# The order of every engine's work written out as a table instead of worked out by a planner

## The chip, the core and the metric

The kernel runs on one core of a Trainium2 chip. A core has a matrix engine (PE, with its weight loads shown as PEld), a vector engine (DVE), a scalar engine (ACT), a general engine (POOL) and a queue engine that issues transfers (SP). Each runs its own list of instructions in order and waits on semaphores for the others. The metric is the device time of one execution in microseconds, lower is better; the times shown are medians.

## The reference, cut to what matters

```python
def reference(**kwargs):
    attn_out = _attn_ref(q, k, v)             # 4 batches, 8 heads, 576 tokens, 64 wide, float32
    x = attn_out.transpose(0, 2, 1, 3).reshape(2304, 512)
    x = _moe_ref(x, w_in, w_out)              # 512 -> 2048 -> 512
    return _moe2_ref(x, w_gate, w_val, w_out, rms_g)   # 512 -> 1536 -> 512

def _attn_ref(q, k, v):
    scores = q @ k.T / sqrt(64)               # a query sees keys of its own and earlier blocks of 64
    attn = softmax(masked scores)
    return attn @ v

def _moe_ref(x, w_in, w_out):
    h = x @ w_in
    return (h * tanh(softplus(h))) @ w_out    # mish

def _moe2_ref(x, w_gate, w_val, w_out, rms_g):
    xn = x / sqrt(mean(x * x) + 1e-6) * rms_g
    g = xn @ w_gate
    return (g * sigmoid(g) * (xn @ w_val)) @ w_out
```

## The kernel before

Most products are made of float16 pairs: a float32 matrix is split into a high and a low half, and three of the four products of halves are added in PSUM (`PASSES`). Three stages overlap. In the first, attention runs tile by tile (`a1_0` is batch 1, tile 0 of 128 tokens): scores `s` (L988, L989 for the mask), their row maxima (DVE L1023), a bias (L1032), the exponential `e` (ACT L1048), a split into halves `p` (L1122, L1125, L1129), a transposing transfer to `pt`, the product with `v` (PE L1162), and a scaled copy `xfl` (DVE L1192) that empties the PSUM tile. In the second stage, interleaved with the first, the mish layer runs in steps of 256 columns by 256 tokens: `h` (PE L1379) into a ring of two PSUM tiles, mish `f` on ACT (L1405), its halves `g` (L1417 or L530 or L1414, then L1422), and `y` (PE L1440). The third stage multiplies `g` and `v` (PE L1841) and `o` (PE L2000) by a seven-product scheme, with sums and differences on DVE or POOL (L1884, L1897) and halves `pp` (L1907, L1908, L1910); its weights are prepared in halves beforehand (L1687 to L1698).

ACT holds one table of functions at a time. Exponential, mish and silu need different ones, so each turn from `e` to `f` or back puts an ACT_TABLE_LOAD into ACT's list.

The code first records 5,150 operations, each with the buffers it reads and writes and one to three alternatives: an engine, a duration in ns, and the function that emits it. Nothing is emitted while recording. `Plan.run` then calls `place`, a list scheduler with a cost model (latencies between engines, table loads, the shared lock of DVE and POOL), and emits the operations in the order of the start times found, each on the engine found; seven tables of numbers shift its priorities. `with_idle` puts fillers before PE operations where the plan has PE idle in the first 60 us: matmuls of zeros that nothing reads (L2086). The order of emission sets the order on every engine, all transfers going through SP.

```python
for o in self.with_idle():
    o.alts[o.pick][2]()
```

Of the kernel before, what the change touches and what calls it, by code (L numbers as in the profile page):

```python
# [26 lines left out]
LAT = {  # L27
    PE: {PE: 0, ACT: 200, DVE: 200, POOL: 240, DMA: 200, NONE: 0},
    ACT: {PE: 153, ACT: 133, DVE: 133, POOL: 180, DMA: 127, NONE: 0},
    DVE: {PE: 131, ACT: 112, DVE: 112, POOL: 160, DMA: 106, NONE: 0},  # L30
    POOL: {PE: 87, ACT: 68, DVE: 68, POOL: 113, DMA: 62, NONE: 0},
    DMA: {PE: 640, ACT: 660, DVE: 660, POOL: 700, DMA: 650, NONE: 0},
    NONE: {PE: 0, ACT: 0, DVE: 0, POOL: 0, DMA: 0, NONE: 0},
}
T_TINY, TINY_AP = 75.0, 52.0
T_DGE, T_DGE_HEADS, T_BUS = 660.0, 720.0, 1250.0
T_DGE_P16, T_DGE_X16, T_DGE_KT, T_DGE_QT, T_DGE_XN = 1330.0, 1330.0, 1450.0, 1370.0, (1400.0, 1950.0)
T_TABLE, TABLE_PULL = 1290.0, 2500.0
WINDOW, HEAT, COOL = 3413.33, 0.9, 0.3
FILL, FILL_SHARE = 60000.0, 0.75  # L40
HOLD = {DVE: 100.0, POOL: 90.0}
# [46 lines left out]


def shares(e, ns):  # L90
    return e == POOL or e == DVE and type(ns) is Shared
# [8 lines left out]
class Plan:  # L100
# [43 lines left out]
    def place(self, key, back=False):  # L144


        ops = self.ops
        n = len(ops)
        free = {e: 0.0 for e in (PE, ACT, DVE, POOL, DMA, NONE)}
        warm, win, busy, bus = True, 0, 0.0, 0.0  # L150
        later = {e: [] for e in free}
        now = {e: {} for e in free}
        table, lock = None, 0.0
        start, end = [None] * n, [0.0] * n
        ready = [[0.0] * len(o.alts) for o in ops]
        wait = [len(o.succ) if back else len(o.deps) for o in ops]

        def arrive(i):
            o = ops[i]
            for z in (o.pick,) if back else (self.picks[i],) if i in self.picks else range(len(o.alts)):  # L160
                e = o.alts[z][0]
                heapq.heappush(later[e], (ready[i][z], key[i], i, z))

        for i in range(n):
            if wait[i] == 0:
                arrive(i)
        left = n
        while left:
            best = None
            for e in free:  # L170
                w, q, f = later[e], now[e], free[e]
                while w and w[0][0] <= f:
                    t, p, i, z = heapq.heappop(w)
                    kind = ops[i].table if e == ACT else shares(e, ops[i].alts[z][1])
                    heapq.heappush(q.setdefault(kind, []), (p + 0.3 * z, i, z))
                first = None
                for kind, h in q.items():
                    while h and start[h[0][1]] is not None:
                        heapq.heappop(h)
                    if h:  # L180
                        pull, t = 0.0, f
                        if back:
                            pass
                        elif e == ACT:
                            pull = 0.0 if kind is None or kind == table else TABLE_PULL
                        elif kind and lock - HOLD[e] > f:
                            t = lock - HOLD[e]
                            pull = t - f
                        if first is None or h[0][0] + pull < first[0]:
                            first = h[0][0] + pull, t, h  # L190
                while w and start[w[0][2]] is not None:
                    heapq.heappop(w)
                if first is not None and (first[1] <= f or not w or first[1] <= w[0][0]):
                    c = (first[1], e, first[2])
                elif w:
                    c = (w[0][0], e, None)
                else:
                    continue
                if best is None or c[:2] < best[:2]:
                    best = c  # L200
            t, e, heap = best
            if heap is not None:
                _, i, z = heapq.heappop(heap)
            elif e in HOLD and not back:
                free[e] = t
                continue
            else:
                _, _, i, z = heapq.heappop(later[e])
            o = ops[i]
            o.pick = z  # L210
            ns = o.alts[z][1]
            if e == ACT and o.table is not None and not back:
                if table is not None and table != o.table:
                    t += T_TABLE
                table = o.table
            start[i], end[i] = t, t + ns
            if not back and shares(e, ns):
                lock = end[i] = max(t + ns, lock + ns - HOLD[e])
            if e == PE and not back:

                x = t
                while ns > 0:
                    while x >= (win + 1) * WINDOW:
                        share = busy / WINDOW if win * WINDOW > FILL else 1.0
                        warm = share > COOL if warm else share > HEAT
                        win, busy = win + 1, 0.0
                    rate = 1.0 if warm else 2.0
                    step = min(ns * rate, (win + 1) * WINDOW - x)
                    x, busy, ns = x + step, busy + step, ns - step / rate
                    if ns < 1e-6:  # L230
                        break
                end[i] = x
            free[e] = end[i]
            if e == DMA:
                free[e] = t + o.issue
                bus = end[i] = max(t + T_BUS + ns - ns.queued, bus) + ns.queued
            left -= 1
            for d in o.deps if back else o.succ:
                j = d.idx
                r = ready[j]  # L240
                if back:
                    r[d.pick] = max(r[d.pick], end[i] + LAT[d.alts[d.pick][0]][e])
                else:
                    for z, a in enumerate(d.alts):
                        r[z] = max(r[z], end[i] + LAT[e][a[0]])
                wait[j] -= 1
                if wait[j] == 0:
                    arrive(j)
        self.length = max(end)
        return start, end  # L250

    def run(self):
        for o in self.ops:
            for d in o.deps:
                d.succ.append(o)
        def inherit(key):

            for i in range(len(self.ops) - 1, -1, -1):
                o = self.ops[i]
                if o.prio < URGENT:  # L260
                    key[i] = min(key[i], o.prio - URGE)
                for d in o.deps:
                    if key[d.idx] > key[i]:
                        key[d.idx] = key[i]
            return key

        key = inherit([o.prio for o in self.ops])
        best = None

        def rounds(key, n):  # L270
            nonlocal best
            for z in range(n + 1):
                start, end = self.place(key)
                if best is None or self.length < best[0]:
                    best = self.length, start, [o.pick for o in self.ops], end, key
                if z < n:
                    _, end = self.place([-t for t in end], True)
                    key = inherit([-t for t in end])

        rounds(key, ROUNDS)  # L280
        if SHIFT:
            self.picks = PICK
            rounds([k + SHIFT.get(o.part, 0.0) + FINE.get(o.idx, 0.0) for k, o in zip(best[4], self.ops)], ROUNDS2)
        self.length, start, picks, end, _ = best
        for i, o in enumerate(self.ops):
            o.start, o.pick, o.end = start[i], picks[i], end[i]
        for o in self.with_idle():
            o.alts[o.pick][2]()

    def with_idle(self):  # L290

        last = 0.0
        for o in sorted(self.ops, key=lambda o: (o.start, o.idx)):
            if o.alts[o.pick][0] == PE:
                if last < FILL:
                    for _ in range(int((o.start - last) * FILL_SHARE / t_mm(128) * (1.0 if last else 0.5))):
                        self.idle()
                last = o.end
            yield o


# [34 lines left out]
def block_attention_mish_mlp_gated_mlp(  # L336
# [16 lines left out]
    P = 128  # L353
    BLK = 64
    NBLK = S // BLK
    NPAIR = H // 2
# [1735 lines left out]
    close_pool("m1")  # L2092


ROUNDS = 20
URGENT, URGE, ROUNDS2 = 3000.0, 50000.0, 0
SHIFT = {
# [244 lines left out]
```

## Time and profile before

| | |
|---|---|
| median of 3 runs | 938.07 us (937.89 to 938.23) |
| profiled execution, first to last instruction (its span) | 935.2 us |
| PE busy | 911.7 us, 97% |
| DVE busy | 804.6 us, 86% |
| ACT busy | 643.0 us, 69% |
| POOL busy | 508.3 us, 54% |
| granted TensorE clock | 1.000 |

The profile gives the profiled execution its span alone; the median lies 2.9 us above it, for what comes before the first and after the last instruction. A matmul counts as busy from its start to the end of its result, and matmuls overlap in the engine, so a short wait between two of them can lie under the tail of the first.

### The profile page before, as it was taken

How to read it: one execution, taken by the hardware profiler on the slowest of the kernel's cores; microseconds unless marked ns; L12 is line 12 of the kernel's file. 1: busy time of each engine (PE TensorE's matmuls, PEld its weight loads, DVE VectorE, ACT ScalarE, POOL GpSimd, SP SyncE). 2: the span in 40 equal slices, each digit the busy share in tenths (PEclk: the TensorE clock that was granted, in tenths of full speed). 3: DMA queues.
4: the chain of work that ended last, by engine and by line, in shares of the span. 5: the costliest groups of instructions: out<-in, count | busy, mean ns of one | idle time of the engine just before them, and what ended most of it. 6: DMA issues, size and time to landing. Idle time of an engine off the chain costs nothing.

```text
span 935.2 us, 20362 instructions
## 1 busy us (share of the span) xinstructions
PE 911.7 (97%) x7395; PEld 622.2 (67%) x7396; DVE 804.6 (86%) x1920; ACT 643.0 (69%) x1330; POOL 508.3 (54%) x644
## 2 busy tenths in 40 slices
PE   8999998999999999999999999999999999999997
PEld 7775567476676766676675665767676676767676
DVE  6899978988786669989874989999999999997676
ACT  4687969899689788887795457667675465463431
POOL 1172548585655526578532749388757577353311
PEclk9999999999999999999999999999999999999999
DMA  9676596888958595898944667736566370716011
GB/s 240 188 232 186 136 172 138 141 146 168 161 117 150 112 169 119 162 184 180 180 71 87 133 184 145 176 76 105 91 187 117 104 131 14 139 21 154 13 69 68
DMA packets 317189, 125.47 MB, mean 134 GB/s; under 512 B 296352, under 2 KB 296352, under 8 KB 317088
## 3 DMA queue, kind: packets, MB, share of 16 engines
q1 hardware_dynamic: 317088, 124.17, 62.6%
q8 instruction: 58, 0.95, 0.4%
q14 instruction: 43, 0.35, 0.1%
HBM read 50.07 MB, written 12.98 MB: 67 GB/s over the span
## 4 chain that ended last, share of the span: by engine, by line
PE 41%; DVE 11%; ACT 5%; POOL 3%; DMA 2%; issue 2%; SPq 0%; DVEq 0%; ACTq 0%; POOLq 0%
PE o L2000 10%; PE y L1440 6%; PE g_u L1841 6%; PE v_u L1841 5%; PE h L1379 4%; PE g L1841 4%; PE v L1841 4%; DMA pt<-p 1%; PE shared L1162 1%; DVE g L1422 1%; DVE mx L1023 1%; ACT e L1048 1%; DVE pp L1910 1%; DVE w2o L564 0%; PE s L988 0%
## 5 line engine op out<-in xcount | busy, mean ns | idle before, releaser
L1379 PE MATMUL h<-x,w1i 128*128 128x256 f16 x1536 | 181.4, 273 | 2.0 <-ACT f L1405 1.8
L1440 PE MATMUL y<-w1o,g 128*128 128x512 f16 x768 | 179.4, 379 | 0.1
L1379 PEld LDWEIGHTS <-w1i 128*128 128x128 f16 x1536 | 145.7, 98 | 25.2 <-issue 3.9
L2000 PE MATMUL o<-w2o,pp 128*128 128x256 f16 x1134 | 138.0, 272 | 1.0 <-POOL pp L1910 0.6
L2000 PEld LDWEIGHTS <-pp 128*128 128x128 f16 x1134 | 110.7, 98 | 23.5 <-issue 1.1
L1440 PEld LDWEIGHTS <-g 128*128 128x128 f16 x768 | 70.4, 98 | 75.4 <-issue 1.7
L1841 PEld LDWEIGHTS <-w2g 128*128 128x128 f16 x756 | 73.8, 98 | 48.1 <-issue 3.8
L1841 PEld LDWEIGHTS <-w2v 128*128 128x128 f16 x756 | 73.9, 98 | 46.0 <-issue 1.8
L1023 DVE TENSOR_REDUCE mx<-s 128x1 f32<-128x512 f32 (+4 forms) x128 | 70.2, 557 | 19.3 <-PE s L989 13.7
L1048 ACT ACTIVATE e<-s,bias,cS 128x512 f32<-128x512 f32 (+4 forms) x120 | 72.6, 607 | 20.1 <-DVE bias L1032 6.9
L1841 PE MATMUL v_u<-xnT,w2v 128*128 128x384 f16 x432 | 81.1, 326 | 0.1
L1841 PE MATMUL g_u<-xnT,w2g 128*128 128x384 f16 x432 | 79.6, 326 | 0.1
L1129 POOL TENSOR_TENSOR p<-e,p 128x384 f16<-128x384 f32 (+4 forms) x60 | 58.6, 977 | 36.4 <-ACT p L1125 19.7
L1422 DVE SCALAR_TENSOR_TENSOR g<-f,ich,g 128x512 f16<-128x512 f32 x64 | 56.7, 886 | 17.1 <-ACT g L1417 10.8
L1841 PE MATMUL g<-xnT,w2g 128*128 128x384 f16 x324 | 61.3, 326 | 1.2 <-DVE sl21g L1878 0.8
L1162 PEld LDWEIGHTS <-pt 128*128 128x128 f16 (+1 forms) x1368 | 44.5, 103 | 26.6 <-issue 10.7
L1841 PE MATMUL v<-xnT,w2v 128*128 128x384 f16 x324 | 61.5, 326 | 0.6 <-DVE u2v L1922 0.6
L1162 PE MATMUL shared<-v,pt 128*128 128x64 f16 (+1 forms) x1368 | 50.5, 195 | 5.5 <-DMA pt<-p 2.6
L1048 ACT ACT_TABLE_LOAD x41 | 52.6, 1283 | 2.5 <-DVE p L1129 1.0
L1405 ACT ACTIVATE f<-h,ch 128x512 f32<-128x512 f32 x64 | 43.4, 685 | 9.2 <-PE h L1379 4.8
L1405 ACT ACT_TABLE_LOAD x38 | 48.8, 1283 | 1.1 <-PE h L1379 0.4
L530 POOL TENSOR_SCALAR p<-e 128x128 f16<-128x128 f32 (+2 forms) x55 | 29.2, 534 | 27.5 <-ACT e L1048 21.1
(351 smaller groups left out, 2070.2 us busy)
## 6 DMA issues: line engine op xcount, KB each, us to landing
wir<-in_moe_w_in_dram SPq DMA_DIRECT2D x16, 512.0 KB, 5.2
wor<-in_moe_w_out_dram SPq DMA_DIRECT2D x16, 512.0 KB, 3.8
w2rg<-in_moe_w_gate_dram SPq DMA_DIRECT2D x24, 256.0 KB, 3.5
w2rv<-in_moe_w_val_dram SPq DMA_DIRECT2D x24, 256.0 KB, 3.3
w2ro<-in_moe_w_out_dram SPq DMA_DIRECT2D x24, 256.0 KB, 2.8
q<-in_q_dram SPq DMA_DIRECT2D x16, 256.0 KB, 3.9
k<-in_k_dram SPq DMA_DIRECT2D x16, 256.0 KB, 4.1
v<-in_v_dram SPq DMA_DIRECT2D x16, 256.0 KB, 3.8
```

What stands on the lines that cost most here:

```text
L530: nc.gpsimd.tensor_scalar(out=out_, in0=in_, scalar1=by, scalar2=1.0, op0=ALU.mult, op1=ALU.mult)
L1023: lambda z=z, cols=cols: nc.vector.reduce_max(out=mx()[:, cols], in_=ts[z](), axis=AX.X),
L1048: lambda y=y, z=z, c0=c0, w=w, acc=acc, e=e, h=h: nc.scalar.activation(out=e()[:, c0 : c0 + w], in_=ts[z]()[:, y, :], func=AF.Exp, bias=bi ...
L1129: lo = lambda eng, z=z, ev=ev: eng.tensor_tensor(out=view(p16)[:, z, :, 1, :], in0=ev(0, kt), in1=view(p16)[:, z, :, 0, :], op=ALU.subtract)
L1162: nc.tensor.matmul(xt()[sl, cols, :], pv(z)[:, t, ph, sl], v16[b, t]()[:, vh, c0 : c0 + D], start=(t == 0 and y == 0), stop=(t == kt - 1 a ...
L1379: nc.tensor.matmul(ph()[:, g, :], w1i[fq]()[:, cc, wh, f * P : (f + 1) * P], x()[:, xh * NCC + cc, :], start=(z == 0), stop=(z == 3 * NCC ...
L1405: ACT, t_act(W, 1, True), lambda: nc.scalar.activation(out=e(), in_=phf(), func=AF.Mish, scale=cs()),
L1422: lambda: nc.vector.scalar_tensor_tensor(out=g16()[:, 1], in0=hv(), scalar=sc(), in1=g16()[:, 0], op0=ALU.mult, op1=ALU.subtract),
L1440: nc.tensor.matmul(yps[t, m](), g16()[:, gh, g, m * P : (m + 1) * P], w1o[f]()[:, wh, :], start=(f == 0 and z == 0), stop=(f == NF1 - 1 an ...
L1841: nc.tensor.matmul(b(), w[wo]()[:, wh, cc, :], x()[:, (2 * xo + xh) * 2 + cc, :], start=(first and i == 0), stop=(i == 5), skip_group_chec ...
L1910: lo = lambda eng: eng.tensor_tensor(out=pp()[:, 1, :], in0=x(), in1=pp()[:, 0, :], op=ALU.subtract)
L2000: nc.tensor.matmul(b()[:, side, :], pps[r][po]()[:, gh, m * P : (m + 1) * P], w[wo]()[:, wh, r, :], start=(first and i == 0), stop=(i == 5 ...
```

## The change

The planner is taken out. `run` walks a table `ORDER` of the 5,150 operation numbers, emits each on the engine that a string `PICKS` names, and puts `IDLE` fillers before eleven of them. The operations, their buffers and their dependencies are the same, except that the ten transposes of `q` and `k` for batch 0 also wait for two constants that the fillers read. Lines of the kernel body stand 167 lines earlier in the changed file (L1379 becomes L1212).

```diff
     def run(self):
-        for o in self.ops:
-            for d in o.deps:
-                d.succ.append(o)
...
-        for o in self.with_idle():
-            o.alts[o.pick][2]()
+
+        for i in ORDER:
+            for _ in range(IDLE.get(i, 0)):
+                self.idle()
+            self.ops[i].alts[int(PICKS[i])][2]()
...
-        op(PE, t_mm(P, 2) * NPAIR, mm, r=[t, ident], w=[tp], at=at)
+        op(PE, t_mm(P, 2) * NPAIR, mm, r=[t, ident, idle_in, ones_h], w=[tp], at=at)
...
+ORDER = (
+    29, 34, 2, 17, 20, 23, 40, 35, 8, 1, 3, 36, 18, 5, 37, 19, 26, 6, 9, 10, 7, 38, 46, 21, 30, 22, 159, 52, 158, 24,
...
+PICKS = (
+    "0000000000000000000000000100000000000000000010000010000010000000000001000000000001000000000000000000"
...
+IDLE = {
+    18: 36, 21: 13, 159: 11, 164: 3, 187: 4, 216: 9, 168: 1, 185: 1, 255: 1, 272: 8, 277: 4,
+}
```

Of the 3,548 operations on DVE, ACT and POOL, 716 change their engine: 264 from POOL to DVE and 186 back, 98 from ACT to DVE and 87 back, 50 from POOL to ACT and 31 back. DVE goes from 1,920 operations to 2,009, POOL from 639 to 542, ACT from 989 to 997. Among the operations recorded for the third stage and its weights alone, DVE goes from 809 to 886 and POOL from 236 to 167. ACT's list has 63 table loads instead of 85. The fillers go from 156 to 91; the first transpose of `q` has 36 ahead of it instead of 25, and from the second attention group on 31 stand in place of 107. Three places follow; in the names, numbers behind the tile's own are buffer numbers.

**SP at the program's start.** Before (`wir` is a raw piece of `w_in`):

```order
L755 DMA q_0_2_88<-in_q_dram 128x8x64
L755 DMA k_0_3_109<-in_k_dram 128x8x64
L755 DMA v_0_7_125<-in_v_dram 128x8x64
L579 DMA wir_0_127<-in_moe_w_in_dram 128x1024
L579 DMA wir_1_129<-in_moe_w_in_dram 128x1024
```

Changed:

```order
L412 DMA wir_0_90<-in_moe_w_in_dram 128x1024
L588 DMA q_0_2_97<-in_q_dram 128x8x64
L588 DMA k_0_3_99<-in_k_dram 128x8x64
L588 DMA k_1_4_101<-in_k_dram 128x8x64
L412 DMA wir_1_103<-in_moe_w_in_dram 128x1024
```

A weight piece now goes ahead of the first queries and keys.

**DVE where batch 0's last attention tile is copied out of PSUM** (`xfl0_4_0`, which reads the tile that batch 1's first product with `v` will write). Before, from the scale of batch 1's `v` on:

```order
L708 TENSOR_SCALAR s2_2309<-E1_496,wor_217_1284,wos_216_2304 128x4
L564 SCALAR_TENSOR_TENSOR v16_1_0_2284<-v1_0_157_1486,sv1_2268,v16_1_0_2284 128x512
L1188 TENSOR_SCALAR r_196_1991<-r_196_1991,fx0_4_2297 128x4
L559 TENSOR_SCALAR w1o0_2321<-wos0_971,s2_2309 128x512
L1192 TENSOR_TENSOR xfl0_4_0_2328<-shared_133,r_196_1991 128x256
```

Changed:

```order
L541 TENSOR_SCALAR s2_2178<-E1_751,wor_217_2172,wos_216_2176 128x4
L1021 TENSOR_SCALAR r_196_2174<-r_196_2174,fx0_4_2159 128x4
L386 TENSOR_TENSOR q16_1_2_1979<-q1_2_225_1746,q16_1_2_1979 128x8x64
L1019 RECIPROCAL r_212_2199<-r0_211_2044 128x4
L1025 TENSOR_TENSOR xfl0_4_0_2201<-shared_114,r_196_2174 128x256
L1255 SCALAR_TENSOR_TENSOR g11_2197<-f11_2108,ich1_1154,g11_2197 128x512
L776 COPY fxd_209_2225<-F2_2098 64x1
L397 SCALAR_TENSOR_TENSOR v16_1_0_2166<-v1_0_157_1494,sv1_2095,v16_1_0_2166 128x512
```

The low half of `v` stood ahead of the copy and now stands behind it, and the weight's high half (L559) is no longer among DVE's rows; on PE, 79 matmuls instead of 25 lie between the square sum of batch 1's `v` and the first product that reads its halves (48 of them of `h`, against 12).

**ACT between two mish steps of the same token tile** (`f25` and `f26`). Before:

```order
L1405 ACTIVATE f25_4110<-h25_4034,ch3_3372 128x512
L1417 ACTIVATE g25_4124<-f25_4110,ich3_3388 128x512
L1478 ACTIVATE sums_b_2995,ss_359_4128<-y2_1_3156,kap2_3386 128x512
L1048 ACT_TABLE_LOAD
L1048 ACTIVATE e2_0_0_4171,sum_345_4172<-s2_0_0_0_4052,bias_344_4130,cS_325_3552 128x128
L1405 ACT_TABLE_LOAD
L1405 ACTIVATE f26_4222<-h26_4087,ch3_3372 128x512
```

Changed:

```order
L1238 ACTIVATE f25_3919<-h25_3855,ch3_2813 128x512
L958 ACTIVATE p16_1_4_2_3849<-e1_4_2_3770 128x128
L1250 ACTIVATE g25_3923<-f25_3919,ich3_3414 128x512
L1311 ACTIVATE sums_b_2962,ss_359_3972<-y2_1_3109,kap2_3512 128x512
L1238 ACTIVATE f26_3998<-h26_3906,ch3_2813 128x512
L1348 ACTIVATE sums_b_2962<-sums_b_2962 128x3x256
L1250 ACTIVATE g26_4027<-f26_3998,ich3_3414 128x512
```

One exponential with a table load on either side stood between the two mish steps; it has moved behind `f27`, to its neighbours.

## Rows read from the trace of the kernel before

**Rows 1.** The page's part on engines: busy us, share of the span, instructions.

```profile
PE 911.7 (97%) x7395; PEld 622.2 (67%) x7396; DVE 804.6 (86%) x1920; ACT 643.0 (69%) x1330; POOL 508.3 (54%) x644
```

**Rows 2.** Busy time by stretch: length, engines (instructions), PE clock, DMA share, GB/s.

```profile
core 0: us, PE busy (x) PEld busy (x) DVE busy (x) ACT busy (x) POOL busy (x), PEclk, DMA share, GB/s
0.00:38.00 38.00, 33.72 (x305) 28.04 (x306) 26.20 (x79) 20.72 (x65) 5.25 (x22) 1.00 0.85 218
38.00:135.00 97.00, 96.83 (x588) 60.09 (x588) 91.25 (x213) 74.81 (x172) 45.58 (x67) 1.00 0.68 183
135.00:250.00 115.00, 108.66 (x1079) 73.03 (x1081) 99.34 (x320) 102.99 (x217) 76.22 (x108) 1.00 0.83 151
250.00:500.00 250.00, 244.79 (x2412) 168.16 (x2407) 202.95 (x560) 207.00 (x393) 136.22 (x199) 1.00 0.74 145
500.00:850.00 350.00, 347.32 (x2428) 234.63 (x2427) 324.56 (x646) 208.45 (x430) 225.84 (x231) 1.00 0.56 115
850.00:936.00 86.00, 80.41 (x599) 58.21 (x596) 60.33 (x106) 29.03 (x55) 19.20 (x18) 1.00 0.20 65
```

**Rows 3.** Waits of PE, whole span: who ended them, us in total, times, longest.

```profile
PE s L988 <- ACT e L1048: 3.3, 9, 0.7
PE shared L1162 <- DMA pt<-p: 2.6, 5, 0.9
PE shared L1162 <- DVE xfl L1192: 2.4, 2, 1.9
...
PE h L1379 <- ACT f L1405: 1.8, 3, 1.1
```

**Rows 4.** PE's groups by form: count, busy us, mean ns of one, idle before.

```profile
L1379 PE MATMUL h<-x,w1i 128*128 128x256 f16 x1536 | 181.4, 273 | 2.0 <-ACT f L1405 1.8
...
L2086 PE MATMUL shared<-idle_in,ones_h 128*128 128x128 bf16 x156 | 14.0, 242 | 2.5 <-DVE idle_in L451 1.9 <-DVE xfl L1192 0.5
```

**Rows 5.** The chain that ended last: start, us, one piece of many matmuls.

```profile
331.55 2.62 PE h L1379 x24
```

**Rows 6.** Timeline at 154 us: start, us, instruction, [idle before it and its releaser].

```profile
153.80 0.95 DVE L564 SCALAR_TENSOR_TENSOR v<-v,sv,v 128x512 f16<-128x512 f32 x1
...
154.98 0.47 DVE L559 TENSOR_SCALAR w1o<-wos,s 128x512 f16<-128x512 f32 x1
155.38 0.41 DVE L1192 TENSOR_TENSOR xfl<-shared,r 128x256 f32<-128x256 f32 x1
...
155.93 0.42 PE L1162 MATMUL shared<-v,pt 128*128 128x64 f16 x9 [1.94 <-DVE xfl L1192]
```

**Rows 7.** Timeline at 258 us, ACT and PE.

```profile
257.70 1.28 ACT L1048 ACT_TABLE_LOAD   x1
...
259.00 0.46 ACT L1048 ACTIVATE e<-s,bias,cS 128x128 f32<-128x128 f32 x1
259.35 0.19 ACT L1048 ACTIVATION_READ_ACCUMULATOR e<-s,bias,cS 128x1 f32 x1
259.56 1.28 ACT L1405 ACT_TABLE_LOAD   x1
...
260.86 1.27 ACT L1405 ACTIVATE f<-h,ch 128x512 f32<-128x512 f32 x2
...
261.60 1.58 PE L1379 MATMUL h<-x,w1i 128*128 128x256 f16 x13 [1.07 <-ACT f L1405]
```

**Rows 8.** The page's groups of table loads on ACT.

```profile
L1048 ACT ACT_TABLE_LOAD x41 | 52.6, 1283 | 2.5 <-DVE p L1129 1.0
...
L1405 ACT ACT_TABLE_LOAD x38 | 48.8, 1283 | 1.1 <-PE h L1379 0.4
```

**Rows 9.** Timeline of PE in the first microseconds.

```profile
1.89 2.83 PE L2086 MATMUL shared<-idle_in,ones_h 128*128 128x128 bf16 x25 [1.89 <-DVE idle_in L451]
...
4.51 1.06 PE L862 MATMUL tpqT<-ident,q 128*128 128x128 f32 x4
```

**Rows 10.** DVE's and POOL's groups by form: third-stage operations of one size.

```profile
L1897 DVE TENSOR_TENSOR sl11g<-sl11g,sl12g 128x384 f32<-128x384 f32 x6 | 4.9, 812 | 0.1
...
L1884 DVE TENSOR_TENSOR sl11g<-c2v,sl11g 128x384 f32<-128x384 f32 x6 | 3.6, 600 | 0.4
```

More of the change, by code (lines that the diff above doesn't have):

```diff
@@ L1 @@
-import heapq
 from contextlib import ExitStack
@@ L25 @@
 PE, ACT, DVE, POOL, DMA, NONE = "PE", "ACT", "DVE", "POOL", "DMA", "NONE"
[L27 to L34, printed above, removed]
 T_TINY, TINY_AP = 75.0, 52.0
-T_DGE, T_DGE_HEADS, T_BUS = 660.0, 720.0, 1250.0
+T_DGE, T_DGE_HEADS = 660.0, 720.0
 T_DGE_P16, T_DGE_X16, T_DGE_KT, T_DGE_QT, T_DGE_XN = 1330.0, 1330.0, 1450.0, 1370.0, (1400.0, 1950.0)
[L38 to L41, printed above, removed]
 class Shared(float):
@@ L87 @@
     __slots__ = ("alts", "prio", "deps", "succ", "wait", "start", "end", "pick", "idx", "part", "table", "issue")
-def shares(e, ns):
-    return e == POOL or e == DVE and type(ns) is Shared
 def split_part(a):
@@ L142, in op @@
         return o
[L144 to L250, printed above, removed]
@@ L252, in run @@
-    def run(self):
-        for o in self.ops:
-            for d in o.deps:
-                d.succ.append(o)
[L256 to L286, printed above, removed]
-        for o in self.with_idle():
-            o.alts[o.pick][2]()
@@ L290, in with_idle @@
[L290 to L299, printed above, removed]
+    def run(self):
+        for i in ORDER:
+            for _ in range(IDLE.get(i, 0)):
+                self.idle()
+            self.ops[i].alts[int(PICKS[i])][2]()
```

60 lines of the change are left out of this document (53 added, 7 removed), and 447 rows, old and new, of tables (FINE, ORDER, PICK, SHIFT).

## Prediction, written before the changed kernel ran

> **What bounds the kernel now.** First the busy shares: PE is busy 911.7 of 935.2 us [rows 1], so no other engine is the bound over the whole span, and 23.5 us of PE idle is what can be seen to win. Then the stretches [rows 2], subtracting PE's busy time from the length of each: 4.3 us idle in 0 to 38, 0.2 in 38 to 135, 6.3 in 135 to 250, 5.2 in 250 to 500, 2.7 in 500 to 850, and 5.6 less the 0.8 us past the span in the last. The first stretch is the start, where nothing has been loaded yet; the last is the end, where the final results drain. What an order can win lies in the three middle stretches: 6.3 + 5.2 + 2.7 = 14.2 us.
>
> That is not all. A matmul of 256 columns lasts 273 ns [rows 4], but 24 of them in a row take 2.62 us, 109 ns each [rows 5]. A wait therefore begins 273 - 109 = 164 ns before PE shows idle, hidden under the last matmul's tail. The four largest groups of waits hold 3.3 + 2.6 + 2.4 + 1.8 = 10.1 us in 9 + 5 + 2 + 3 = 19 waits, 0.53 us each [rows 3]. At that size 14.2 us are 27 waits, which hide another 27 x 0.164 = 4.4 us. So 18.6 us stand in waits that another order could shorten: 15.1 us between 135 and 500 (11.5 idle, 22 waits, 3.6 hidden) and 3.5 us between 500 and 850 (2.7 idle, 5 waits, 0.8 hidden).
>
> The timelines then say what these waits are. The longest, 1.94 us, ends with DVE's copy `xfl` at 155.38, and DVE had not been idle: it ran the low half of `v` (0.95 us) and the high half of a weight (0.47 us) first, both needed later [rows 6]. Another, 1.07 us at 261.60, ends with a mish step on ACT; ACT had loaded a table (1.28 us), done one exponential, and loaded the other table again [rows 7]. Both are waits behind work in an engine's own list that could have stood elsewhere, and this is what an order decides.
>
> **The change, part by part.** *PE's own work*: the same matmuls, so nothing, apart from the fillers.
>
> *Start.* A weight piece of 128 x 1024 floats, 512 KB, goes ahead of `q`; at the 218 GB/s of the first stretch [rows 2] that is up to 2.4 us. The fillers ahead of the first transpose took 2.83 us for 25, 113 ns each, and it began at 4.51 [rows 9]; 36 take 4.1 us from 1.89 on, to 5.96, so the transpose comes at least 1.5 us later. In return 65 fillers fewer stand on PE. All 156 hold 14.0 us [rows 4], 0.090 us each: 5.8 us if they stand in the way of work, nothing if PE would have waited there anyway. Ends: +2.4 and 2.4 - 5.8 = -3.4. I take 0: the later start is certain, and the attention chain behind it has fewer fillers to pass.
>
> *Table loads.* 22 fewer on ACT, 1.283 us each [rows 8]: 28.2 us of ACT time. ACT is not the bound, but it is 103.0 of 115 us busy between 135 and 250 [rows 2], where PE waits most. Each load in front of a mish step or an exponential delays what PE needs next, at most by its own 1.28 us; here it shows in the waits for `f` and `e`, 1.8 and 3.3 us [rows 3]. In this kernel the exponential ends at 259.54, the load begins at 259.56 and the next operation at 260.86, 20 ns behind the load's end [rows 7]: nothing but the 1.28 us. The Trainium skill (ScalarE: Activation LUTs, "What ACT_TABLE_LOAD costs") counts 2.66 us for a switch, a load of 1283 ns and a drain of about 1380. By that the 22 would free 58.5 us of ACT; the trace shows the load and no drain, and the trace decides.
>
> *Order on DVE and ACT.* At the first wait neither half stands ahead of `xfl` any more, so 0.95 + 0.47 us of the 1.94 go [rows 6], and on PE 79 matmuls instead of 25 lie between the square sum of `v` and the product that needs its halves; at 109 ns [rows 5] the 36 more of `h` alone are 3.9 us of cover. At the second both loads and the exponential, 260.86 - 257.70 = 3.2 us [rows 7], are gone from in front of `f26`, three times the wait. Unknown is how many new waits the other order makes. From below, all 15.1 us between 135 and 500 go; from above, none. I take two thirds, 10.1 us: the places looked at lose all or most of their wait, and new short ones will take part of it back. Of the 3.5 us in the third stage I likewise take two thirds, 2.3.
>
> *POOL to DVE.* In the third stage and its weights DVE gets 77 operations more and POOL 69 fewer. At the stretch's means, 324.56 / 646 = 0.502 us and 225.84 / 231 = 0.978 us [rows 2], DVE gets 38.7 us and POOL loses 67. DVE is already 324.6 of 350 us busy, so this would make 363, more than there is. But its operations there are stretched: two sums of 128 x 384 floats take 812 ns in one group and 600 in another [rows 10]. If up to 26% of DVE's time, 85 us, is such waiting for POOL, 67 / 225.8 = 30% less POOL gives 25 back: 324.6 + 38.7 - 25 = 338 us, 97% of the stretch, hidden under PE's 347 but without much reserve. I charge 0.8 us of new PE waits. The Trainium skill (SBUF — State Buffer, "SBUF: two separate sides") bears on it: DVE and POOL share a port pair under an exclusive lock, the loser blocks for the whole instruction, so less POOL work would let DVE go faster. The unequal prices agree, though they don't show which operation held the lock.
>
> *Sum:* 0 - 10.1 - 2.3 + 0.8 = -11.6 us. The span goes from 935.2 to 923.6; with the 2.9 us between span and median that makes 926.5.
>
> **Rivals.** *All waits go and the start gets shorter.* For it: at the places read, the moved work exceeds the wait. Against: waits at other places are shorter than 0.5 us and need not have one cause. 938.1 - 18.6 - 3.4 = 916; taken as 914 to 920.
>
> *The waits only move.* For it: PE is 97% busy, and every operation moved ahead puts another one back. Then the time stays within 2 us, 938.
>
> *DVE becomes the bound of the third stage* (slower). Its price: without the relief 363 us for the 350 us stretch, and at the 812 ns of rows 10 for each of the 77 it would be 324.6 + 62.5 = 387. That is 13 to 37 us past the stretch, less the 10.1 won earlier: 941 to 965, at the middle 953. It decides once DVE's busy time there passes PE's 347. Against it: the 67 us taken from POOL.
>
> *The start is later and nothing makes up for it, or PE's clock falls.* The clock is 1.00 (2.4 GHz) throughout [rows 2], with 107 fillers from the second attention group to the first mish step; 31 remain. PE's own work in the first stretch is 33.7 - 14.0 = 19.7 us [rows 2, 4]; at 1.2 GHz it would take up to 19.7 us more, of which PE's waits would absorb some. With +2.4 alone the sum is -9.2; it is slower only if the clock is low for more than about 12 us of that work.
>
> **How the numbers follow.** The forecast, 920 to 932, gets 0.58; all waits gone 0.15; a smaller gain, 932 to 936, 0.06; waits moved 0.08; DVE as the bound 0.09; the clock 0.04. A measurement tells 0.2%, 1.9 us, from no change. Faster: 0.58 + 0.15 + 0.06 = 0.79; the same: 0.08; slower: 0.13. The range runs from 914, the end of the better rival, to 939, which takes in the moved waits, and leaves out the DVE and clock cases and some of the ends, less than 2 in 10. The likeliest case alone is 920 to 932.
>
> **What would show it.** In the stretch from 135 to 500 PE's idle falls from 11.5 us to about 4, and the waits for `xfl` and `f` leave the list's head. The table loads number 63 and ACT's busy time falls by some 25 us. In the third stage DVE's share rises to about 97% while PE stays at 99%; POOL's falls by about 67 us. The first transpose stands near 6 to 7 us, the first mish step (first reading `x` of tile 0) still near 38. Wrong would be: DVE at 100% with PE waiting for it, a granted clock under 1.00 before 40 us, or an idle time of PE between 135 and 500 that is no smaller.

## The result, and the profile after

The changed kernel takes 924.94 us (median of four executions, 923.66 to 926.21), before takes 938.15 beside it; the ratio is 0.9855, 95% interval 0.9836 to 0.9874. The forecast was 926.5: by the medians the change won 13.2 us, 1.6 more than the 11.6 of the prediction's sum. All rows below come from one profiled execution of each kernel, with spans of 935.2 and 923.7 us, 11.5 apart. In every execution whose time and span are both on record the time lies 1.7 to 1.9 us above the span, so the profiled execution of before took about 937.0 us, 1.1 below its median; that of after took 925.54, 0.6 above its own. The total thus came out near the sum. Its terms did not; most of what follows is about that.

The busy line of the page, to be read beside [rows 1]:

```profile
PE 902.4 (98%) x7329; PEld 617.7 (67%) x7331; DVE 782.2 (85%) x2009; ACT 612.1 (66%) x1316; POOL 400.7 (43%) x547
```

ACT is 30.9 us less busy, POOL 107.6 us less, and DVE 22.4 us less although it has 89 operations more. The stretches, to be read beside [rows 2]:

```profile
0.00:38.00 38.00, 30.55 (x243) 24.75 (x245) 23.49 (x55) 19.41 (x67) 6.84 (x22) 1.00 0.76 205
38.00:135.00 97.00, 95.35 (x562) 58.59 (x562) 88.58 (x210) 76.69 (x178) 48.42 (x77) 1.00 0.71 187
135.00:250.00 115.00, 109.75 (x1085) 74.62 (x1084) 101.80 (x321) 98.92 (x209) 60.92 (x96) 1.00 0.82 145
250.00:500.00 250.00, 248.41 (x2479) 170.14 (x2478) 196.51 (x598) 193.58 (x393) 113.25 (x172) 1.00 0.75 143
500.00:850.00 350.00, 348.95 (x2458) 240.07 (x2457) 320.70 (x734) 199.10 (x425) 150.96 (x160) 1.00 0.59 121
```

PE idles 5.3 + 1.6 = 6.8 us between 135 and 500, where it idled 11.5. Between 500 and 850 its idle time only falls from 2.7 to 1.1 us. But PE does different work at the same time in the two traces, so idle time in fixed stretches cannot say where the 11.5 us between these two executions were won. For that I gave each matmul the usual distance to the next one of its shape (the lower quartile over both traces; fillers nothing), summed what was still to come at a time, and subtracted after from before:

```
at us                   38   135   180   250   350   500   550   600   700   850   900
work ahead, us         0.6   0.7   0.0   2.1   3.1   6.1   7.0   9.9   9.3  11.1  11.0
```

So nothing up to 180 us, then 6 us by 500, another 4 in the hundred microseconds in which the mish layer ends and the third stage begins, and about 1 more up to 850.

PE's waits (us in total, times, longest), to be read beside [rows 3]:

```profile
PE shared L1919 <- DVE idle_in L284: 6.3, 1, 6.3
PE shared L995 <- DMA pt<-p: 2.3, 4, 1.0
PE s L821 <- ACT e L881: 1.5, 4, 0.8
PE shared L995 <- DVE xfl L1025: 1.5, 2, 1.0
```

The waits for `f` are gone and those for `e` are about half; `xfl` is still there, at other places, and the wait for `pt` is nearly what it was. At the head stands a new wait at the start. The table loads of the two main lines (busy us, mean ns), [rows 8]:

```profile
L881 ACT ACT_TABLE_LOAD x30 | 38.5, 1283 | 2.1 <-DVE bias L865 1.2 <-DVE ich L1193 0.2 <-DVE sum L890 0.2
L1238 ACT ACT_TABLE_LOAD x27 | 34.6, 1283 | 2.0 <-issue 1.0 <-DVE g L1255 0.6
```

The start in the timeline (start, length, what), [rows 9]:

```profile
0.72 0.39 SPq L412 DMA_DIRECT2D wir<-in_moe_w_in_dram  x1
5.25 0.69 DVE L429 TENSOR_SCALAR cv<-wir 128x512 uint32<-128x512 uint32 x1 [5.25 <-DMA wir<-in_moe_w_in_dram]
6.12 0.11 DVE L284 MEMSET idle_in<- 128x64 uint32 x1
6.28 2.93 PE L1919 MATMUL shared<-idle_in,ones_h 128*128 128x128 bf16 x26 [6.28 <-DVE idle_in L284]
10.07 1.04 PE L695 MATMUL tpqT<-ident,q 128*128 128x128 f32 x4
```

DVE's list now begins with a weight conversion that waits for a transfer until 5.25 us; the fill of the constant that the fillers read stands behind it, so the fillers start at 6.28 instead of 1.89 and the first transpose at 10.07 instead of 4.51. The first mish step nevertheless starts at 37.35 us, no later than before.

The place of `xfl0_4_0` in the timeline, [rows 6]:

```profile
151.68 0.39 DVE L1025 TENSOR_TENSOR xfl<-shared,r 128x256 f32<-128x256 f32 x1
152.76 0.73 DVE L397 SCALAR_TENSOR_TENSOR v<-v,sv,v 128x512 f16<-128x512 f32 x1
153.54 0.19 PE L995 MATMUL shared<-v,pt 128*128 128x64 f16 x1 [0.27 <-DVE v L397]
```

The copy is done at 152.07, and of a wait of 1.94 us 0.27 is left, now for the low half of `v`.

### The profile page after: what moved, and what is told of

Same layout as the page of the kernel before. It is cut to its first block, busy times and chain, and to the rows that moved or that the text cites. A ratio compares the mean times of both kernels' runs of the same rounds, so it can differ in the third digit from the quotient of the medians.

```text
span 923.7 us, 20213 instructions
## 1 busy us (share of the span) xinstructions
PE 902.4 (98%) x7329; PEld 617.7 (67%) x7331; DVE 782.2 (85%) x2009; ACT 612.1 (66%) x1316; POOL 400.7 (43%) x547
## 4 chain that ended last, share of the span: by engine, by line
PE 82%; DVE 7%; DMA 5%; ACT 2%; issue 2%; POOL 1%; SPq 0%; DVEq 0%; ACTq 0%; POOLq 0%
PE h L1212 15%; PE y L1273 14%; PE o L1833 12%; PE g_u L1674 7%; PE v_u L1674 7%; PE v L1674 5%; PE g L1674 5%; PE shared L995 3%; PE h L1203 3%; PE y L1281 3%; DMA pt<-p 2%; PE s L816 2%; PE s L821 2%; DMA k<-in_k_dram 1%; PE s L839 1%
## 5 line engine op out<-in xcount | busy, mean ns | idle before, releaser
L1212 PE MATMUL h<-x,w1i 128*128 128x256 f16 x1536 | 180.3, 273 | 0.0
L1212 PEld LDWEIGHTS <-w1i 128*128 128x128 f16 x1536 | 146.2, 98 | 24.2 <-issue 2.7
L1833 PE MATMUL o<-w2o,pp 128*128 128x256 f16 x1134 | 140.3, 273 | 0.5 <-DVE acc_xf L1854 0.2
L881 ACT ACTIVATE e<-s,bias,cS 128x512 f32<-128x512 f32 (+4 forms) x120 | 72.5, 606 | 32.4 <-DVE bias L865 17.2
L962 POOL TENSOR_TENSOR p<-e,p 128x384 f16<-128x384 f32 (+4 forms) x43 | 40.4, 941 | 40.5 <-ACT p L958 17.8
L1255 DVE SCALAR_TENSOR_TENSOR g<-f,ich,g 128x512 f16<-128x512 f32 x64 | 52.1, 816 | 2.5 <-ACT g L1250 2.0
L962 DVE TENSOR_TENSOR p<-e,p 128x512 f16<-128x512 f32 (+4 forms) x69 | 38.2, 554 | 10.2 <-ACT p L958 4.3
L865 POOL TENSOR_SCALAR bias<-mx,nS 128x1 f32<-128x1 f32 (+1 forms) x43 | 22.7, 528 | 34.1 <-DVE mx L856 24.2
```

The lines of the kernel that those rows point to most:

```text
L881: lambda y=y, z=z, c0=c0, w=w, acc=acc, e=e, h=h: nc.scalar.activation(out=e()[:, c0 : c0 + w], in_=ts[z]()[:, y, :], func=AF.Exp, bias=bi ...
L962: lo = lambda eng, z=z, ev=ev: eng.tensor_tensor(out=view(p16)[:, z, :, 1, :], in0=ev(0, kt), in1=view(p16)[:, z, :, 0, :], op=ALU.subtract)
L1212: nc.tensor.matmul(ph()[:, g, :], w1i[fq]()[:, cc, wh, f * P : (f + 1) * P], x()[:, xh * NCC + cc, :], start=(z == 0), stop=(z == 3 * NCC ...
L1255: lambda: nc.vector.scalar_tensor_tensor(out=g16()[:, 1], in0=hv(), scalar=sc(), in1=g16()[:, 0], op0=ALU.mult, op1=ALU.subtract),
L1833: nc.tensor.matmul(b()[:, side, :], pps[r][po]()[:, gh, m * P : (m + 1) * P], w[wo]()[:, wh, r, :], start=(first and i == 0), stop=(i == 5 ...
```

## Experiments

My theory (A): PE waits for operations that stood behind other work in an engine's list, and the order takes these waits away, each where it stood. Against it: the gain is the work taken off POOL (B); order and engines only fit each other (C); the waits only move (D). The kernel before, timed beside each set, had medians of 938.2 to 939.1 us and single executions from 935.9 to 941.9, so differences under 2 us between sets are not read. Where an expectation names other theories, its letters are its own.

**One half of the program at a time.** In effect, with each operation on the engine of the table that placed it:

```diff
-        for i in ORDER:
+        for i in ORDER[:3053] + [j for j in ORDER_BEFORE if j not in ORDER[:3053]]:
```

> The new order and engines up to 505 us, where after's last mish product of token tile 7 is through, and those of before for the rest. Theory A (the gain is the sum of waits taken away, each where it stood): the remaining work of TensorE was 6 to 7 us ahead at this point, so 931 to 932 us. Theory D (the waits only move: a third stage in the old order gives the lead back): 936 to 938 us. ACT table loads are 63 here as in after, so if loads alone made the gain it would be 925 to 927.

Measured: 929.64 us, ratio 0.9893 (0.9872 to 0.9914). The work ahead is 8.0 us at 550 and still 8.0 at 850: the old third stage gives nothing back. The other half, with the first 3,058 entries of the old order:

> The order and engines of before up to 511 us, the new ones for the rest. Theory A: the lead grows by 4 to 5 us behind that point, so 933 to 934 us, though the table loads are 85 as before. Theory D (the third stage is short of waits only because the new first part prepares it): 937 to 939 us. My forecast for this part was 1.5 us, which would give 936.6.

Measured: 932.87 us, ratio 0.9937 (0.9916 to 0.9958). In its profiled execution the first half, in the order and on the engines of before, ran 3.1 us behind the profile of before; up to 1.7 us of that is a lower granted clock (0.50 from 158 to 160 us, 0.70 from 160 to 162); from 550 to 850 the work ahead rises from -3.1 to 1.5, by 4.6 us. The two gains, 10.0 and 5.9 us by their ratios, add up to 15.9 against 13.6 for both together, within the intervals of about 2 us each. D is out between the halves, and the third stage's gain is its own, with 85 table loads in place. No run separates order from engines within that stage alone.

The same stage in the two orders also shows DVE. VectorE groups between 500 and 850 us (busy us, mean ns), first with the old third stage (POOL 225 us busy there):

```profile
L1743 DVE TENSOR_TENSOR pp<-sl11g,pp 128x384 f16<-128x384 f32 x14 | 11.4, 817 | 1.8 <-ACT pp L1741 1.8
L1755 DVE SCALAR_TENSOR_TENSOR u2v<-v,ck,u2v 128x384 f32<-128x384 f32 x15 | 9.2, 611 | 0.7 <-PE v L1674 0.6
```

and in the kernel after (POOL 151 us busy):

```profile
L1755 DVE SCALAR_TENSOR_TENSOR u2v<-v,ck,u2v 128x384 f32<-128x384 f32 x15 | 9.2, 614 | 4.1 <-PE v L1674 3.9
L1743 DVE TENSOR_TENSOR pp<-sl11g,pp 128x384 f16<-128x384 f32 x14 | 9.1, 647 | 0.5 <-ACT pp L1741 0.4
```

The subtraction with both inputs in SBUF falls from 817 to 647 ns; the operation that reads `v` from PSUM stays at 611 to 614. Taken one by one, all of DVE's `pp` subtractions in this stage show why: in the kernel before, 40 of the 44 run while POOL works and last 896 ns on average, the other 4 last 552; in the kernel after, 20 of 57 run while POOL works and last 692, the other 37 last 551. `u2v`, from PSUM, lasts 603 to 619 ns in either case.

**Order and engine choices apart.** All 716 choices back, in the new order with its fillers; in effect:

```diff
-PICKS = PICKS_AFTER
+PICKS = PICKS_BEFORE
```

> The new order and its fillers, with the 716 engine choices of before. Theory A (the order takes waits away, the engines matter little): most of the 13.2 us stay, 925 to 930 us. Theory B (the work taken from POOL makes DVE faster, and that is the gain): at least two thirds of it go, 934 us or more. Theory C (order and engines fit only each other): slower than before, over 940 us, with PE waiting for operations that are back on POOL.

Measured: 990.92 us, ratio 1.0548 (1.0521 to 1.0576). The reverse, the old order and fillers with the new choices:

> The order and fillers of before, with the 716 new engine choices. Theory A: 936 to 941 us, no gain to speak of. Theory B: 925 to 930 us, and POOL busy near 400 us in place of 508. Theory C: over 940 us.

Measured: 989.80 us, ratio 1.0531 (1.0504 to 1.0559), with POOL at 403 us busy. A misses by 61 and 49 us; the first run alone would pass B, which set no upper end there, but in the second, with POOL relieved, B misses by 60. C holds for the times: POOL's relief alone is no gain, and neither is the order. The sign that C named shows only one step back. PE's longest waits in the new order with the old engines are for ACT and DVE, while ACT's waits for a bias on POOL hold 26.0 us there and 14.8 in after:

```profile
PE s L821 <- ACT e L881: 10.2, 13, 2.3
PE g_u L1674 <- DVE sl11g L1755: 6.7, 8, 2.4
PE shared L995 <- DVE xfl L1025: 3.6, 4, 2.1
PE g_u L1674 <- DVE sl22g L1755: 3.3, 4, 2.1
```

**A few choices of work with time to spare.** Only the preparation of the third stage's weights goes back to its old engines; in effect:

```diff
-            self.ops[i].alts[int(PICKS[i])][2]()
+            old = self.ops[i].part.startswith(("rg", "rv", "2w"))
+            self.ops[i].alts[int((PICKS_BEFORE if old else PICKS)[i])][2]()
```

> The kernel after with the third stage's weight preparation alone back on the engines of before (136 choices, 64 of them from VectorE back to POOL); no result of it is wanted soon. Theory A (less POOL work is what shortens VectorE's operations): POOL's busy time in 500 to 850 us rises by 35 to 55 us, VectorE's falls by less than the work that leaves it, and its two-operand sums from SBUF last 650 to 800 ns each; the time rises by 0 to 3 us, 925 to 928. Theory B (order and engines fit only each other, whatever the slack): 940 us or more, with PE waiting for the v_u and g_u operands.

Measured: 942.67 us, ratio 1.0053 (1.0033 to 1.0073), 17.7 us over after: the time that its theory B gave, and mine, A, fell. POOL rose by 30 us between 500 and 850, DVE's `pp` stayed at 646 ns, but PE idled 12.6 us there: 5.5 us for operands of `g_u` and `v_u`, as B had it, and 4.5 us for copies that empty the PSUM tiles of `o`. The longest wait of this stage, in the timeline:

```profile
645.97 0.90 POOL L1531 TENSOR_TENSOR w2sg<-w2fg 128x256 f32<-128x256 f32 x1
646.90 0.42 ACT L1520 ACTIVATE w2g<-w2sg 128x256 f16<-128x256 f32 x1 [2.41 <-POOL w2sg L1531]
647.23 0.60 ACT L1702 ACTIVATE sl22g<-sl22g,cg 128x384 f32<-128x384 f32 x1
648.10 0.46 ACT L1847 ACTIVATE acc_xf<-o,co 128x256 f32<-128x256 f32 x1
648.62 0.60 PE L1833 MATMUL o<-w2o,pp 128*128 128x256 f16 x4 [1.94 <-ACT acc_xf L1847]
```

PE shows no wait for the weights themselves, but the weight half `w2g` stands in ACT's list ahead of `acc_xf`, which empties a PSUM tile that PE wants. POOL was late with `w2sg`, ACT stood for 2.41 us, and PE for 1.94. A list is in order: what has time to spare has none for those behind it. How much of the other waits has this cause was not read.

**Table loads.** Eleven one-column exponentials in the kernel after, each ahead of a mish step (`DETOUR`, from 140 to 467 us), bring the loads back to 85:

```diff
+            if i in DETOUR:
+                self.detour()
...
+    plan.detour = lambda: nc.scalar.activation(out=spare(), in_=ones()[:, 0:1], func=AF.Exp)
```

> The kernel after with 11 one-column exponentials on ACT, each just ahead of a mish step that followed another mish step, spread from 140 to 467 us: 22 more table loads of 1.28 us each, 85 as in before, and nothing else. Theory A (ACT has room, the loads are a small part of the gain): each costs at most part of its 2.8 us, at the 77 to 86% that ACT is busy there about a quarter of 28 us is the upper end, so 926 to 930 us. Theory B (the loads were the gain of the first part): 6 us or more, 931 to 938. Theory C (an order this tight cannot bear any delay): over 940, PE waiting for f at most of the eleven places.

Measured: 943.63 us, ratio 1.0069 (1.0045 to 1.0094). The control, with the same operations as mish:

> As the run with 22 more loads, but the eleven one-column operations are mish instead of exponentials, so that no table is loaded: 63 loads, 11 operations of about 0.2 us more. Theory A (the 18.7 us of that run were the table loads): 924 to 927 us. Theory B (any further operation in ACT's list does it): 935 us or more.

Measured: 925.41 us, ratio 0.9851 (0.9836 to 0.9866). So the operations cost nothing that can be told and the loads (943.63 - 925.41) / 22 = 0.83 us each, with all that they set off. That is more than A and B allowed, and PE waits for `e`, not for `f` as C had it (two lines were added, so L883 is L881 of after):

```profile
PE s L823 <- ACT e L883: 16.6, 12, 3.0
```

The same eleven in the kernel before:

> The order and engines of before with 11 one-column exponentials, each just ahead of a mish step that followed another mish step, from 141 to 467 us: 22 more table loads, 107 in place of 85. Theory A (a load between mish and exponential costs time in either order, 18.7 / 22 = 0.85 us each): 952 to 960 us. Theory B (only the new order is that sensitive, since its waits are gone; the old one has waits that swallow the loads): 938 to 945.

Measured: 962.66 us, ratio 1.0249 (1.0228 to 1.0269); one of four executions lasted 5361 us for a reason that nothing here shows and is left out. (962.66 - 938.73) / 22 = 1.09 us each. The old order is as sensitive as the new one, and there was hardly any slack that would swallow a load: here PE does wait for `f`.

```profile
PE h L1214 <- ACT f L1240: 11.1, 11, 1.9
```

Part of this price is the clock's. In the run of the old order (the third number from the right is the granted clock):

```profile
188.00:190.00 2.00, 0.80 (x5) 0.41 (x5) 0.75 (x1) 1.98 (x5) 0.47 (x1) 1.00 0.30 64
190.00:192.00 2.00, 1.42 (x6) 0.50 (x4) 0.44 (x2) 1.99 (x5) 0.79 (x3) 0.55 0.32 52
192.00:194.00 2.00, 2.00 (x10) 0.87 (x8) 1.83 (x6) 1.16 (x6) 1.90 (x3) 0.59 0.50 72
194.00:196.00 2.00, 2.00 (x18) 1.50 (x17) 1.77 (x9) 1.82 (x5) 1.07 (x2) 1.00 0.63 114
```

After waits of PE the clock fell to its lower level for a few microseconds. It did so near 160 us too, and in the new order near 152 and 190 us (a third fall there, near 100 us, comes before the first inserted load; that profiled execution took 947.26 us, 3.6 above its median). Added up over such rows the clock withheld at most 3.4 us behind the inserted loads in either run, so at most some 0.15 us of each load's price. With order or engines alone it fell three times, at most 5.1 us of some 52.

**The two places of the prediction, mended by hand in the kernel before:**

```diff
 for the order of before, at two places:
-v16_1_0 (low half), r, w1o0 (high half), xfl0_4_0
+r, xfl0_4_0, v16_1_0 (low half), w1o0 (high half)
...
-f25, g25, e2_0_0, p16 of e2_0_0, f26, f27, g26, e2_0_2
+f25, g25, f26, f27, g26, e2_0_0, p16 of e2_0_0, e2_0_2
```

> Before, with the two places of my prediction mended by hand and nothing else: xfl and its scale moved ahead of the low half of v and of the weight's high half on VectorE; the exponential and its halves that stood between f25 and f26 moved behind g26, two table loads fewer, 83. Theory A (a wait goes with what stood ahead of it): at the first place 0.5 us, since the product needs the low half of v too, at the second 1.07 + 0.16 = 1.2 us; the lead of TensorE's work over before is 0.5 us at 165 us and 1.7 us at 300, the time 936 to 937. Theory B (waits only move): no lead at 300 us. Theory C (an order cannot be changed at one place): a lead below -1 us, 939 or more.

Measured: 938.34 us, ratio 0.9995 (0.9983 to 1.0006). PE's waits from 140 to 170 us:

```profile
PE shared L995 <- DVE xfl L1025: 0.8, 1, 0.8
PE s L821 <- ACT e L881: 0.6, 1, 0.6
PE shared L995 <- DVE v L397: 0.3, 1, 0.3
```

and from 250 to 300:

```profile
PE s L821 <- ACT e L881: 1.2, 2, 0.8
PE shared L995 <- DMA pt<-p: 0.6, 1, 0.6
```

At the first place 1.94 us became 0.8 + 0.3; at 165 us the work ahead was 1.1 us, at 210 it was nothing again. At the second the wait for `f`, 1.07 us, is gone, and the waits for `e` have gone from 0.2 to 1.2 us and those for `pt` from nothing to 0.6: it seems that the exponential that I moved back was wanted too. The work ahead there goes from 0.0 to -0.9. For these two places D is right.

**The start.** The constants' fills ahead of the conversion in DVE's list of the kernel after:

```diff
-    29, 34, 2, 17, 20, 23, 40, 35, 8, 1, 3, 36, 18, 5, 37, 19, 26, 6, 9, 10, 7, 38,
+    29, 34, 2, 17, 20, 23, 40, 1, 3, 8, 5, 6, 9, 10, 7, 35, 36, 18, 37, 19, 26, 38,
```

> The kernel after, with the eight constants' fills placed ahead of the first weight conversion in VectorE's list, so that the fillers no longer wait until 6.28 us for them. They start near 1.5 us and the first transpose moves from 10.07 to about 6 us. Theory A (the start is bound by the attention chain): the first mish step moves up from 37.4 us and the time falls by 2 to 4 us, to 921 to 923. Theory B (the start is bound by the first transfers and by VectorE's weight conversions, or the later waits take it up): the step stays within 1 us of 37.4 and the time within 1 us of 925.

Measured: 921.05 us (920.60 to 923.59), ratio 0.9825 (0.9804 to 0.9846): A, and the best version here. In its timeline:

```profile
1.11 3.81 PE L1919 MATMUL shared<-idle_in,ones_h 128*128 128x128 bf16 x36 [1.11 <-DVE idle_in L284]
6.57 0.63 PE L695 MATMUL tpqT<-ident,q 128*128 128x128 f32 x4 [1.66 <-DMA q<-in_q_dram]
33.44 1.78 PE L1203 MATMUL h<-x,wis 128*128 128x256 f32 x7
```

The first mish step is 3.9 us earlier (33.44 for 37.35), and so is the end (921.05 for 924.94). Of this, 3.5 us are the earlier start of the first transposes (6.57 for 10.07) and 0.4 their length, 0.63 us for 1.04. Without any fillers:

```diff
-IDLE = {18: 36, 21: 13, 159: 11, 164: 3, 187: 4, 216: 9, 168: 1, 185: 1, 255: 1, 272: 8, 277: 4}
+IDLE = {}
```

> The kernel after without its 91 fillers. Theory A (the clock holds without them and they stand where PE waits anyway): 924 to 926 us, granted clock 1.00 from 10 us on. Theory B (the fillers keep the clock up): a granted clock under 1.00 somewhere in the first 40 us and 3 to 20 us more, 928 to 945.

Measured: 936.96 us, ratio 0.9983 (0.9970 to 0.9995), 12.0 us over after. The profile prints a granted clock of 1.00 all along, but the rows say otherwise. PE groups by shape from 20 to 50 us without fillers:

```profile
L985 PE MATMUL shared<-v,pt 128*128 128x64 f32 x48 | 11.3, 412 | 0.0
L816 PE MATMUL s<-kT,qT 64*128 64x256 f32 x16 | 9.6, 710 | 0.3 <-ACT e L881 0.3
```

and in the kernel after from 20 to 35 us:

```profile
L985 PE MATMUL shared<-v,pt 128*128 128x64 f32 x45 | 6.3, 275 | 0.1
L816 PE MATMUL s<-kT,qT 64*128 64x256 f32 x15 | 5.1, 423 | 0.0
```

Matmuls of 128 x 256 floats start 427 ns apart up to 53.5 us and 216 ns apart from there: PE had run at 1.2 GHz until then. That is B, though the column that I named for it shows nothing. Last, the transpose's 1.66 us for `q` in the version with constants first:

```diff
-    29, 34, 2, 17, 20, 23, 40,
+    29, 2, 17, 20, 34, 23, 40,
```

> The kernel with the constants first, and also the first weight piece moved behind the first queries and keys in the queue. Theory A (the transpose waited 1.66 us for q, and what it gains the whole chain gains): first transpose near 5 us, 919 to 920 us. Theory B (the weight conversions, now later, take it up): 921 to 923.

Measured: nine of ten executions between 937.3 and 943.6 us, one 921.84. The transpose did start at 4.36 us. In the timeline of one of the nine:

```profile
9.71 0.63 ACT L456 ACTIVATE junk<-wis 128x512 bf16<-128x512 f32 x1 [4.11 <-DVE wis L445]
10.25 0.58 ACT L699 ACTIVATE kT<-tpkT 128x512 f32<-128x512 f32 x1
10.88 0.79 PE L816 MATMUL s<-kT,qT 64*128 64x128 f32 x2 [4.14 <-ACT kT L699]
```

ACT's list has a square of the weight ahead of `kT`. With the weight later, ACT stood for 4.11 us and PE for 4.14, and the stretches (granted clock 1.00 in the first 10 us) say what that set off:

```profile
10.00:20.00 10.00, 9.12 (x40) 6.51 (x40) 3.86 (x7) 3.04 (x11) 1.80 (x5) 0.53 0.89 253
30.00:40.00 10.00, 10.00 (x36) 6.88 (x36) 5.61 (x9) 4.83 (x19) 1.42 (x3) 0.50 0.25 66
60.00:70.00 10.00, 10.00 (x52) 8.33 (x50) 8.93 (x18) 7.53 (x14) 4.64 (x5) 1.00 0.40 125
```

The clock, at its upper level when the transposes ran (four in 0.60 us), fell to half after the idle time and stayed there past 50 us. The execution of 921.84 us has a mean granted clock of 1.000, the nine others 0.975 to 0.982. Neither A nor B, but the list in order again: what waited stood ahead of what was wanted. A version with that square moved behind `kT` too was not tried.

## Why the prediction came out right, step by step

*What the waits hold, 135 to 500 us: 10.1 of 15.1 us.* Mis-sized: the work ahead rose by 6.1 - 0.7 = 5.4 us there, 36% and not two thirds. With each wait measured as the distance between two matmuls less the shortest tenth of its pair of shapes, 33 waits with idle time held 16.5 us there, where I had 22 with 15.1, and after 17 still hold 9.1, for `pt`, `e` and `xfl` above all; delays of more than 10 ns without idle time did not shrink (9.0 and 10.1 us). What failed is the share of two thirds, taken from two places that were read.

*500 to 850 us: 2.3 us less 0.8.* Mis-sized the other way: 11.1 - 6.1 = 5.0 us. Two steps failed. I counted the 164 ns under a matmul's tail only for waits that show idle time, and took these to be 5. Measured as above, there are 12 such waits with 4.6 us, and 36 delays of more than 10 ns, all short of the tail, with 2.2 us that show no idle time at all; after, 4 with 1.7 and one with 0.05. And the 0.8 us charged for DVE were not due: I forecast it 338 us busy and it is 320.7, at 92% and not 97%. The relief was not 25 us but 324.6 + 38.7 - 320.7 = 42.6, since POOL lost 75 us there and not 67.

*Start: 0.* Right in the sum (0.6 us at 38), wrong in the way: "36 take 4.1 us from 1.89 on" left out what stands ahead of the fillers' constant on DVE. The transpose came at 10.07, not at 6 to 7, and one more look at DVE's first row would have shown it. It was worth 3.9 us, as the run with constants first shows. Nor was the clock 1.00 throughout, as I read it from the column: four transposes take 1.06 us at 4.51 [rows 9] and four others 0.61 at 13.21 in the same trace, so PE began at its lower level.

*Table loads.* The count (63), the 1.28 us and ACT's fall (30.9 us, forecast some 25) held. What I made of them was too little, for they had no term of their own in the sum: 22 loads inserted cost 18 us in the new order and 24 in the old, at most 3.4 of them by the clock, more than the whole first half gained. That their absence pays for the first half, and other rows give part of it back, fits these numbers but is argued: the inserted loads stand where no planner had counted them, and taking two out by hand brought nothing. It stays open how the 5 to 10 us of the first half divide between loads and the rest.

*The two places.* At the first the wait went as read, at the second too; as the cause of the gain they don't stand. Done alone in the old order they gain nothing; at the second place other waits came in its stead.

*The sum.* -11.6 came from 0, -10.1, -2.3 and +0.8; measured -0.6, -5.4 and -5.0, with the rest at the end. An error of 4.7 us one way met one of 3.5 and one of 0.6 the other way: the number was right by more luck than its working. The 2.9 us from span to median were too many as well: 1.8 us lie outside the span, and 1.1 were the profiled execution, faster than the median; with 1.8 the same sum gives 925.4.

*The rivals.* "All waits go" failed: PE idles 6.8 us between 135 and 500. "The waits only move" is refuted for the whole and right for the two places tried. "DVE becomes the bound" failed, since the operations got shorter with POOL's relief. The Trainium skill (SBUF — State Buffer, "SBUF: two separate sides") counts DVE operations with two SBUF inputs among those that contend with POOL for a lock; the trace agrees, some 550 ns alone and 692 to 896 beside POOL for such a one, and 603 to 619 either way for one with an input from PSUM. Once risen, the clock did not fall here, but that case was nearer than its 4 in 100: without fillers 12 us, with one idle time of 4.1 us at the start some 20.

## What to carry to other kernels

An order and its engine choices are one object: either alone cost 5%, and a fifth of the changed choices, of work that PE never waited for, cost more than the whole change had gained. Each list is in order, and the longest of the waits that came stood behind such work. So judge a reordering by the work still to come at a time, by halves and with controls, not by a place where a wait vanishes; and read what stands ahead of the first thing that each engine waits for, which here was worth more than any place in the middle.

## What was not expected of the hardware

A table load, inserted in pairs ahead of mish steps, costs the kernel 0.83 to 1.09 us against its own 1.28, although ACT is only two thirds busy over the span; at most some 0.15 us of that is the clock, which fell after the waits. A DVE subtraction of two SBUF inputs lasts 551 ns alone and 692 to 896 on average beside POOL, one with a PSUM input 603 to 619 either way. Without fillers the granted clock in the profile is 1.00 while matmuls take twice their time up to 53.5 us, so matmul rows, not that column, tell the clock at a program's start. A clock that had fallen after 4.1 us of idle at the start came back only after more than 40 us in which PE was busy 9.1 to 10.0 of every 10, while in the run with more loads in the old order it was back at 1.00 from 194 us on after a fall near 190; what makes the difference is open.
